# Four late-stage changes: order of the fold's first steps, engine of its high parts, theta's due time and conversion buffers

## The chip, the cores and the metric

One core of one Trainium2 chip runs the whole program in one launch. The metric is the time of the program on the device in microseconds (us). The core has a matmul engine (TensorE, PE in the profile, with its weight loads as PEld), VectorE (DVE), ScalarE (ACT), GpSimd (POOL), and SyncE (SP), which here issues nearly all transfers between memory (HBM) and the on-chip buffer SBUF. Matmuls write into PSUM, a small buffer that VectorE and ScalarE read.

## The reference

Two batches, 768 tokens, 8 heads of 64, model width 512. The three functions run one after the other on `x`; cut to what is computed:

```python
def _attn_ref(q, k, v, proj):
    ...
    q_bits = (np.einsum('bhsd,dk->bhsk', q, proj) > 0).astype(np.int64)
    k_bits = (np.einsum('bhsd,dk->bhsk', k, proj) > 0).astype(np.int64)
    powers = 2 ** np.arange(n_bits)
    q_bucket = np.sum(q_bits * powers, axis=-1)
    k_bucket = np.sum(k_bits * powers, axis=-1)
    mask = q_bucket[:, :, :, None] == k_bucket[:, :, None, :]
    scores = scale * np.matmul(q, k.transpose(0, 1, 3, 2))
    scores = np.where(mask, scores, -1000000000.0)
    scores = scores - np.max(scores, axis=-1, keepdims=True)
    attn = np.exp(scores)
    attn = attn / (np.sum(attn, axis=-1, keepdims=True) + 1e-09)
    return np.matmul(attn, v).astype(np.float32)

def _moe_ref(x, w_ch1, w_ch2):
    X = np.fft.fft(x, axis=1)
    X = np.fft.fft(X, axis=2)
    u = x + np.real(X).astype(np.float32)
    ...
    un = (u - mu) / np.sqrt(var + 1e-06)
    ch = np.maximum(un @ w_ch1, 0.0) @ w_ch2
    return (u + ch).astype(np.float32)

def _moe2_ref(x, w_theta, w_tok_r, w_tok_i, w_ch):
    theta = x @ w_theta
    zr, zi = x * np.cos(theta), x * np.sin(theta)
    y = np.einsum('ts,bsd->btd', w_tok_r, zr) + np.einsum('ts,bsd->btd', w_tok_i, zi)
    u = x + y
    return (u + np.maximum(u @ w_ch, 0.0)).astype(np.float32)
```

The MLP's and the second mixer's weights come as float64.

## The kernel before

The program is one stream of work for two batches of six tiles of 128 tokens each. First comes the attention of batch 0, in four pairs of heads (`attention_first`). Its last pair's second half is normalised by `pair_norm` into a PSUM piece `hi`, and ScalarE copies that to `x`. Then batch 0 goes through the transform (class `Fft`), the layernorm and the first MLP product (`mlp1`), while the attention of batch 1 runs beside it (48 tiles of scores, `exp`, transposes and products with `v`); then batch 0's second product (`mlp2`) and its `theta`, the same transform and MLP for batch 1, and last the second mixer of both batches: `theta(1, ...)`, the token sums `tok_sum` and the channel products `tok_out`, in halves of 384 tokens.

Most products are split: an operand is kept as a high and a low part (`xh`, `xl`; `w1h`, `w1l`), and three matmuls replace one.

The transform works on folded inputs. `fold` (l.568) adds and subtracts the upper and lower token tiles of `x` into `fm` (named `fa` in the trace), then column halves, and `part` (l.553) makes each of the pieces `z2`, `e`, `o`, `z0`: the sum or difference into PSUM (for the last pair of heads) or into `zraw`, a high part by ScalarE and a low part by VectorE. `fold` is a generator: each `yield` hands over to the attention's own steps. `rest` (l.614) then runs the matmuls with the tables `ct`, `sn` and `dt`, adds the results into `u`, and swaps two lone columns of each upper tile through a buffer `lone` (l.701 to 703). The layernorm of `u` follows, then `mlp1`.

Float64 weights are converted on the chip by `from_f64` (l.170): SyncE loads a slab of 512 (or 384) columns into a buffer `r64` (`r` in the trace); ScalarE makes two passes over it, VectorE joins the halves by a shift and an or; then ScalarE copies the high part and GpSimd subtracts to get the low part. The buffers come from a pool `cv` of three, in rotation (the list `cvs`). So are made `w1`, `w2`, the token weights (`conv_tok`: 12 tiles of 384 columns for each half, ten of them in the space of `w1`, the last two in `wtx`) and the channel weights `wch` (four tiles).

`theta` (l.814) takes each token tile: four transposes into PSUM, a copy `xs` that is stored to memory for `tok_sum`, the parts `xh` and `xl`, twelve matmuls, then range reduction, sine and cosine on the other engines. `tok_sum` (l.864) adds over 72 matmuls for each 128 channels; `tok_out` (l.886) does the last product, and stores.

What sets the order: each piece of code runs under a priority in microseconds, `at(us)`, or `timed(generator, t0, dt)` that gives the generator's steps the priorities t0, t0 + dt and so on. A scheduler places instructions by these, and by their dependencies; after that every engine runs its instructions strictly in that order, and SyncE's transfers are issued in such an order too. The numbers stand in the table `T` (l.93). Nearly every instruction is issued through one helper, so the trace names line 62 (or 64 for work whose order is kept as written) for all of them; they are told apart by their tiles' names.

Of the kernel before, what the change touches and what calls it, by code (L numbers as in the profile page):

```python
# [33 lines left out]
def f(t):  # L34
    return t.bitcast(F32)
# [35 lines left out]
def fused_kernel(ctx, tc, A, out):  # L71
# [15 lines left out]
    def stt(eng, out, in0, in1, op, scale=1.0):  # L87
# [8 lines left out]
        w2=100.0, w2s=1.0, m0=170.0, f1=190.0, th=240.0, m1=290.0, z0=330.0, wt=300.0, n0=8, n1=16, k0=12, k1=16, c1=46, i0=40, i1=[20, 10],  # L96
# [29 lines left out]
    def PS1():  # L126
        return PS(now[0])
# [262 lines left out]
    def pair_norm(j, part, o, hi=None):  # L390
# [8 lines left out]
        if hi is not None:  # L399
            AC.activation(out=x, in_=hi, func=AF.Copy)  # L400
# [54 lines left out]
    def attention_first(pace, after):  # L455
# [7 lines left out]
        def av(n):  # L463
# [5 lines left out]
            if i == NT - 1:  # L469
                hi = PS("m")[:, 0:384].rearrange("p (t a c) -> p t a c", t=3, a=2) if j == 3 and part else None  # L470
                pair_norm(j, part, o[0], hi)
                if part:
                    slow.append(after(j, hi))
# [57 lines left out]
    class Fft:  # L531
# [23 lines left out]
        def part(self, nm, c, op, a, b, psum=False):  # L555
# [9 lines left out]
            AC.activation(out=hl[:, 0], in_=r, func=AF.Copy)  # L565
            V.tensor_tensor(out=hl[:, 1], in0=r, in1=f(hl[:, 0]), op=ALU.subtract)

        def fold(self, p, hi=None):
# [11 lines left out]
            if hi is not None:  # L580
                fl = PS1()[:, 0:384].rearrange("p (a n) -> p a n", a=6)
# [35 lines left out]
        def rest(self):  # L617
# [64 lines left out]
            for t in range(3):  # L682
# [19 lines left out]
                AC.activation(out=mid, in_=u[:, 3 + t, 448:191:-256], func=AF.Copy)  # L702
                AC.activation(out=u[:, 3 + t, 192:449:256], in_=mid, func=AF.Copy)
# [110 lines left out]
    def theta(b, wth, zt):  # L814
        x2 = u_t[b]
        for t in range(NT):
# [4 lines left out]
            xs = zt([128, 4, 128], F32, "xs")  # L821
            AC.activation(out=xs, in_=pt.rearrange("p (k n) -> p k n", k=4), func=AF.Copy)
            SY.dma_start(out=xTd[b][:, :, c], in_=xs)
# [4 lines left out]
            V.tensor_tensor(out=xl, in0=pk, in1=f(xh), op=ALU.subtract)  # L828
            xx = (xh, xl)
# [59 lines left out]
    def tok_out(b, half, wch, kx):  # L889
# [3 lines left out]
        for m in range(4):  # L893
# [7 lines left out]
            if m % 2:  # L901
                SY.dma_start(out=out[b, 128 * m - 128:128 * m + 128, c].rearrange("(k p) t -> p k t", p=128),
                             in_=xt[:, m - 1:m + 1])
# [23 lines left out]
    attention_first(T["pace0"], lambda j, hi: ft0.fold(PO[j], hi))  # L927
# [100 lines left out]
    w2_p.release()  # L1028
    z1_p = pool("z1")
# [14 lines left out]
    timed(theta(1, wth, zt), t0, 1)  # L1044
# [25 lines left out]
    timed(tok_out(0, 1, wch, k1), t0 + 100, 1)  # L1070
    for p in (xt1_p, wc_p, zb_p, u1_p, xt_p, wx_p, z1_p, dr_p, ring["f"][0][0], ring["m"][1][0], ring["m"][0][0], w1_p, x_p, u0_p, cv_p, const):
        p.release()
# [101 lines left out]
```

## Time and profile before

| what | value |
|---|---|
| time, median of three runs | 740.17 us (737.42, 740.17, 740.52) |
| the profiled execution | 742.22 us |
| its span in the trace | 740.5 us |
| PE busy | 672.8 us, 91% |
| DVE busy | 401.4 us, 54% |
| ACT busy | 376.4 us, 51% |
| POOL busy | 371.2 us, 50% |
| chain that ended last | PE 42%, issue 10%, POOL 10%, DMA 9%, ACT 6%, DVE 4% |

The span is the time from the first to the last thing that the profiler recorded of this one execution; the execution's own time is a little longer. A row of the timeline has the start, the duration, the engine, the line, the operation and its tiles (output, arrow, inputs), and, where the engine was idle before it, how long and who released it. Idle time of an engine counts only where the work that ends last waits for it; in this kernel that is mostly TensorE's.

### The profile page before, as it was taken

The page shows a single profiled execution, that of the slowest core. Times are in us where ns is not written, and L with a number is a line of the kernel's source. Part 1 is how long each engine was busy: PE and PEld are TensorE (multiplying, and loading weights), DVE is VectorE, ACT ScalarE, POOL GpSimd, SP SyncE. Part 2 cuts the span into 40 slices and gives each one's busy share as a digit, 9 for nine tenths or more (in the row PEclk, how much of TensorE's full clock was granted, in tenths as well). Part 3 has the DMA queues.
Part 4 walks back from the last instruction along what each step waited for, and adds up shares of the span by engine and source line. Part 5 has one row for each costly group of instructions (what it writes and reads, how often), then busy time and mean ns, then how long its engine had stood idle before and what let it go on. Part 6 is the DMA issues. An engine that isn't in the chain of part 4 may idle for free.

```text
span 740.5 us, 13468 instructions
## 1 busy us (share of the span) xinstructions
PE 672.8 (91%) x5424; PEld 515.0 (70%) x5424; DVE 401.4 (54%) x649; ACT 376.4 (51%) x603; POOL 371.2 (50%) x312
## 2 busy tenths in 40 slices
PE   5798988778868897999999999999999799989997
PEld 2365566666747654786687675686584798989997
DVE  1466777778899556642394871254321366552222
ACT  2465554867898788764222260354325555562000
POOL 2777879589687888885450110134313155831000
PEclk9999999969789999999999999999999999999999
DMA  9886867469799999786550160010005511561202
GB/s 331 183 167 145 154 115 143 97 176 202 194 227 232 237 235 263 153 142 117 107 175 1 29 165 1 15 43 15 1 2 152 181 44 30 178 185 49 86 1 85
DMA packets 161438, 93.69 MB, mean 127 GB/s; under 512 B 137056, under 2 KB 147552, under 8 KB 161376
## 3 DMA queue, kind: packets, MB, share of 16 engines
q1 hardware_dynamic: 159440, 86.27, 49.9%
q0 software_dynamic: 1936, 6.57, 2.5%
q8 instruction: 42, 0.69, 0.4%
q14 instruction: 20, 0.16, 0.1%
HBM read 49.82 MB, written 6.29 MB: 76 GB/s over the span
## 4 chain that ended last, share of the span: by engine, by line
PE 42%; issue 10%; POOL 10%; DMA 9%; ACT 6%; DVE 4%; SPq 0%; POOLq 0%; ACTq 0%; DVEq 0%
PE psm L62 28%; PE psf L62 10%; DMA r<-in_wtok 4%; DMA r<-in_w 2%; POOL w1l L62 2%; ACT r L62 2%; POOL p L62 2%; PE pss L62 2%; POOL pt L62 2%; PE pso L62 2%; DMA r<-in_wch 1%; DMA x<-p 1%; ACT p L62 1%; ACT stk L62 1%; POOL w2l L62 1%
## 5 line engine op out<-in xcount | busy, mean ns | idle before, releaser
L62 PE MATMUL psm<-unT,w1h 128*128 128x256 f16 x768 | 130.1, 274 | 1.6 <-DVE u L62 1.4
L62 DVE SCALAR_TENSOR_TENSOR r<-r 128x512 uint32<-128x512 uint32 (+1 forms) x64 | 66.7, 1047 | 73.3 <-ACT r L62 61.4
L62 PE MATMUL psm<-unT,w1l 128*128 128x256 f16 x384 | 105.1, 274 | 0.0
L62 PEld LDWEIGHTS <-w1h 128*128 128x128 f16 (+1 forms) x774 | 75.2, 98 | 17.2 <-issue 6.3
L62 POOL TENSOR_TENSOR w1l<-r,w1h 128x384 fp32r<-128x384 f32 (+1 forms) x36 | 41.4, 1163 | 59.0 <-ACT w1h L62 58.9
L62 PEld LDWEIGHTS <-hh 128*128 128x128 f16 x384 | 36.9, 98 | 42.7 <-issue 1.1
L62 ACT ACTIVATE r<-r,chalf 128x512 uint32<-128x512 uint32 (+1 forms) x64 | 46.1, 721 | 38.3 <-DMA r<-in_wtok 20.5
L64 PE MATMUL pss<-stk 64*128 64x384 f32 (+1 forms) x288 | 58.4, 492 | 5.9 <-ACT p L64 3.0
L62 PE MATMUL pss<-stk 128*128 128x384 f32 x192 | 50.0, 388 | 11.9 <-ACT stk L62 6.6
L62 POOL TENSOR_TENSOR p<-p,p 128x768 f16<-128x768 f32 x32 | 53.4, 1672 | 12.9 <-ACT p L62 11.4
L62 PE MATMUL psm<-w2h,hl 128*128 128x512 f16 x192 | 59.7, 380 | 0.0
L62 PE MATMUL psm<-w2l,hh 128*128 128x512 f16 x192 | 59.4, 379 | 0.0
L62 PE MATMUL psm<-w2h,hh 128*128 128x512 f16 x192 | 59.3, 380 | 0.0
L62 DVE TENSOR_REDUCE nm<-pss 128x1 f32<-128x768 f32 x48 | 44.9, 946 | 20.5 <-PE pss L62 20.4
L64 DVE TENSOR_REDUCE nm<-pss 128x1 f32<-128x768 f32 x48 | 43.6, 950 | 22.5 <-PE pss L64 22.5
L62 ACT ACTIVATE p<-pss,nm 128x768 f32<-128x768 f32 x48 | 42.7, 895 | 21.7 <-DVE nm L62 20.2
L62 DVE SCALAR_TENSOR_TENSOR hl<-psm,hh 128x512 f16<-128x512 f32 x48 | 32.9, 685 | 37.8 <-ACT hh L62 37.7
L62 ACT ACTIVATE hh<-psm 128x512 f16<-128x512 f32 x48 | 28.3, 590 | 46.5 <-PE psm L62 46.4
L62 PEld LDWEIGHTS pss<-stk 128*128 128x128 f32 x192 | 35.3, 209 | 15.8 <-ACT stk L62 7.7
L62 PEld LDWEIGHTS <-w1l 128*128 128x128 f16 x384 | 37.6, 98 | 6.4 <-issue 1.7
L62 ACT ACTIVATE r<-r 128x512 f32<-128x512 f32 (+1 forms) x64 | 39.6, 619 | 0.0
L62 POOL TENSOR_SCALAR nn<-nn 128x512 f32<-128x512 f32 x12 | 8.3, 691 | 60.9 <-ACT nn L62 60.9
(319 smaller groups left out, 1583.8 us busy)
## 6 DMA issues: line engine op xcount, KB each, us to landing
r<-in_w SPq DMA_DIRECT2D x32, 512.0 KB, 4.9
r<-in_wtok SPq DMA_DIRECT2D x24, 384.0 KB, 3.8
vr<-in_v SPq DMA_DIRECT2D x8, 390.0 KB, 3.7
stk<-stk SPq DMA_DIRECT2D x16, 192.0 KB, 3.7
xT<-xs SPq DMA_DIRECT2D x12, 256.0 KB, 2.6
xt<-xT SPq DMA_DIRECT2D x4, 768.0 KB, 5.1
out<-xt SPq DMA_DIRECT2D x8, 384.0 KB, 2.5
ct<-in_ct POOLq DMA_DIRECT2D x4, 579.0 KB, 7.7
```

The costliest lines, as they stand in the source:

```text
L62: return fn(*a, **k)
L64: self.last = fn(*a, **k)
```

## The change

Eight edits, in four groups.

1. **Fold of batch 0's last pair.** `pair_norm` no longer issues the copy of `hi` to `x` itself but returns it as `back`; `fold` issues it after its first two additions. In `part`, where the piece is in PSUM (this pair only: four pieces), VectorE makes the high part, and ScalarE no longer does.
2. **Lone columns.** For batch 0 and its first tile the two copies of the swap are VectorE's.
3. **Tail.** In `theta`, the copy `xs` and its store are written behind `xh` and `xl`. The priorities of `theta(1, ...)` are 16 us earlier (`tp=16`). After the second MLP's weights are released, a pool `cv3` of three more buffers joins `cvs`, so that conversions from then on rotate over six. The program's ring for software DMA is 4096 bytes per partition where it had the default (`dynamic_dma_scratch_size`).
4. **End.** The last `tok_out` stores each 128 channels by itself (four stores of 128x384) where it stored two at a time.

```diff
@@ T = dict(...
-        ... k0=12, k1=16, c1=46, i0=40, i1=[20, 10],
+        ... k0=12, k1=16, c1=46, tp=16, i0=40, i1=[20, 10],
@@ pair_norm
-        if hi is not None:
-            AC.activation(out=x, in_=hi, func=AF.Copy)
+        return lambda: AC.activation(out=x, in_=hi, func=AF.Copy)
@@ attention_first, av
-                pair_norm(j, part, o[0], hi)
+                back = pair_norm(j, part, o[0], hi)
                 if part:
-                    slow.append(after(j, hi))
+                    slow.append(after(j, hi, back))
@@ class Fft, part
-            AC.activation(out=hl[:, 0], in_=r, func=AF.Copy)
+            if psum:
+                V.tensor_copy(out=hl[:, 0], in_=r)
+            else:
+                AC.activation(out=hl[:, 0], in_=r, func=AF.Copy)
             V.tensor_tensor(out=hl[:, 1], in0=r, in1=f(hl[:, 0]), op=ALU.subtract)
-        def fold(self, p, hi=None):
+        def fold(self, p, hi=None, back=None):
...
             yield
             if hi is not None:
+                back()
                 fl = PS1()[:, 0:384].rearrange("p (a n) -> p a n", a=6)
@@ class Fft, rest
-                AC.activation(out=mid, in_=u[:, 3 + t, 448:191:-256], func=AF.Copy)
-                AC.activation(out=u[:, 3 + t, 192:449:256], in_=mid, func=AF.Copy)
+                if self.b or t:
+                    AC.activation(out=mid, in_=u[:, 3 + t, 448:191:-256], func=AF.Copy)
+                    AC.activation(out=u[:, 3 + t, 192:449:256], in_=mid, func=AF.Copy)
+                else:
+                    V.tensor_copy(out=mid, in_=u[:, 3 + t, 448:191:-256])
+                    V.tensor_copy(out=u[:, 3 + t, 192:449:256], in_=mid)
@@ theta
-            xs = zt([128, 4, 128], F32, "xs")
-            AC.activation(out=xs, in_=pt.rearrange("p (k n) -> p k n", k=4), func=AF.Copy)
-            SY.dma_start(out=xTd[b][:, :, c], in_=xs)
             xh = zt([128, 4, 128], F32R, "xh")
             xl = zt([128, 4, 128], F32R, "xl")
             pk = pt.rearrange("p (k n) -> p k n", k=4)
             AC.activation(out=xh, in_=pk, func=AF.Copy)
             V.tensor_tensor(out=xl, in0=pk, in1=f(xh), op=ALU.subtract)
+            xs = zt([128, 4, 128], F32, "xs")
+            AC.activation(out=xs, in_=pt.rearrange("p (k n) -> p k n", k=4), func=AF.Copy)
+            SY.dma_start(out=xTd[b][:, :, c], in_=xs)
@@ tok_out
-    def tok_out(b, half, wch, kx):
+    def tok_out(b, half, wch, kx, last=False):
...
-            if m % 2:
+            if last:
+                SY.dma_start(out=out[b, 128 * m:128 * m + 128, c], in_=xt[:, m])
+            elif m % 2:
@@ the tail, after the second MLP
     w2_p.release()
+    cv3_p = pool("cv3", 3)
+    cvs += [cv3_p] * 3
...
-    timed(theta(1, wth, zt), t0, 1)
+    timed(theta(1, wth, zt), t0 - T["tp"], 1)
...
-    timed(tok_out(0, 1, wch, k1), t0 + 100, 1)
+    timed(tok_out(0, 1, wch, k1, True), t0 + 100, 1)
@@ building the program
-    nc = _bacc.Bacc("TRN2", target_bir_lowering=False, num_devices=1)
+    nc = _bacc.Bacc("TRN2", target_bir_lowering=False, num_devices=1, dynamic_dma_scratch_size=4096)
```

The changed program's order of instructions on each engine differs from the old one's at many places. Three of them are shown, each before and after. A row has the source line, the operation, the output tile, an arrow, the input tiles and the size; the number behind a tile's name only tells tiles apart.

**First batch's `u` on VectorE.** `psm_2066` is the transform's result for tile 0, `u_1888` is batch 0's `u`, `r64_...` are weights under conversion, `nm_...` and `bits_...` belong to the second batch's attention, `bs_...` are the layernorm's statistics. Before:

```order
L62 SCALAR_TENSOR_TENSOR r64_1933<-r64_1933 128x512
L64 TENSOR_TENSOR fa_1986<-psm_2039,fa_1986 128x386
L64 TENSOR_TENSOR hlz2_2063<-psm_2053,hlz2_2063 128x384
L62 TENSOR_SCALAR bits_2697<-pss_2698 64x768
L62 SCALAR_TENSOR_TENSOR r64_1940<-r64_1940 128x512
L64 TENSOR_TENSOR u_1888<-u_1888,psm_2066 128x512 x2
L62 TENSOR_REDUCE nm_2714<-pss_2709 128x1
L62 SCALAR_TENSOR_TENSOR r64_1947<-r64_1947 128x512
L64 TENSOR_TENSOR u_1888<-un0_113,psm_2087 1x512
L64 BN_STATS bs_2104<-u_1888 128x6
```

After:

```order
L62 SCALAR_TENSOR_TENSOR r64_1933<-r64_1933 128x512
L64 TENSOR_TENSOR hlz2_2063<-psm_2053,hlz2_2063 128x384
L64 TENSOR_TENSOR u_1888<-u_1888,psm_2066 128x512 x2
L62 SCALAR_TENSOR_TENSOR r64_1940<-r64_1940 128x512
L64 TENSOR_TENSOR u_1888<-un0_113,psm_2087 1x512
L62 TENSOR_SCALAR bits_2697<-pss_2698 64x768
L62 TENSOR_REDUCE nm_2673<-pss_2668 128x1
L64 COPY lone_2098<-u_1888 128x2
L62 SCALAR_TENSOR_TENSOR r64_1947<-r64_1947 128x512
L62 TENSOR_REDUCE nm_2714<-pss_2709 128x1
L64 COPY u_1888<-lone_2098 128x2
L64 BN_STATS bs_2104<-u_1888 128x6
```

The two additions into `u` stand ahead of the shift of `r64_1940` and of one step of the attention; the two copies of the lone columns are new on this engine, with a shift and a reduction between them.

**The second batch's theta on TensorE.** `psm_6592` and `psm_6593` are the last results of the second MLP (weights `w2h`, `w2l`), `psm_6975` a token sum, `psf_6738` (after: `psf_6741`) theta's tile 0, with `xh_6734` and `xl_6735`. Before, the last rows of 29 matmuls of the token sum that stand between the MLP and theta:

```order
L62 MATMUL psm_6975<-w1l_6521,x_5416 128x384
L62 MATMUL psm_6975<-w1h_6520,za_5417 128x384
L62 MATMUL psm_6975<-w1h_6520,zb_5418 128x384
L62 MATMUL psm_6975<-w1l_6521,zb_5418 128x384
L62 MATMUL psf_6738<-wthh_5386,xh_6734 128x512
L62 MATMUL psf_6738<-wthl_5387,xh_6734 128x512
L62 MATMUL psf_6767<-ident_93,u1_5032 128x128 x3
L62 MATMUL psf_6738<-wthh_5386,xl_6735 128x512
```

After:

```order
L62 LDWEIGHTS hh_6302
L62 MATMUL psm_6593<-w2l_2190,hh_6302 128x512
L62 LDWEIGHTS hl_6303
L62 MATMUL psm_6592<-w2h_2189,hl_6303 128x512
L62 MATMUL psf_6741<-wthh_5386,xh_6734 128x512
L62 MATMUL psf_6741<-wthl_5387,xh_6734 128x512
L62 MATMUL psf_6770<-ident_93,u1_5032 128x128 x2
L62 MATMUL psf_6741<-wthh_5386,xl_6735 128x512
```

Theta's tile 0 has moved from behind the MLP and 29 matmuls of the token sum into the MLP's last group.

**The same place on VectorE and SyncE.** `u1_5032` is the second batch's `x` of the mixer; its two additions take the MLP's last results. `r64_6585` to `r64_6722` are token weights, the `r64_71..` of 512 columns are channel weights. VectorE before:

```order
L62 SCALAR_TENSOR_TENSOR r64_6585<-r64_6585 128x384
L62 SCALAR_TENSOR_TENSOR r64_6712<-r64_6712 128x384
L62 SCALAR_TENSOR_TENSOR r64_6719<-r64_6719 128x384
L62 SCALAR_TENSOR_TENSOR u1_5032<-psm_6592,u1_5032 128x512
L62 SCALAR_TENSOR_TENSOR u1_5032<-psm_6593,u1_5032 128x512
L62 TENSOR_TENSOR xl_6735<-psf_6726,xh_6734 128x512
L62 SCALAR_TENSOR_TENSOR r64_7143<-r64_7143 128x512
L62 SCALAR_TENSOR_TENSOR r64_7150<-r64_7150 128x512
```

VectorE after:

```order
L62 TENSOR_TENSOR xl_6776<-psf_6770,xh_6775 128x512
L62 SCALAR_TENSOR_TENSOR rr_6757<-nn_6754,psf_6741 128x512
L62 SCALAR_TENSOR_TENSOR rr_6757<-nn_6754,rr_6757 128x512
L62 SCALAR_TENSOR_TENSOR r64_7146<-r64_7146 128x512
L62 SCALAR_TENSOR_TENSOR r64_7153<-r64_7153 128x512
L62 TENSOR_SCALAR nn_6754<-rr_6757 128x512
L62 SCALAR_TENSOR_TENSOR rr_6757<-rr_6757,u1_5032 128x512
L62 SCALAR_TENSOR_TENSOR r64_7160<-r64_7160 128x512
L62 SCALAR_TENSOR_TENSOR rr_6798<-nn_6795,psf_6782 128x512
L62 SCALAR_TENSOR_TENSOR u1_5032<-psm_6592,u1_5032 128x512
L62 SCALAR_TENSOR_TENSOR u1_5032<-psm_6593,u1_5032 128x512
```

SyncE before:

```order
L62 DMA r64_6585<-in_wtok 128x768
L62 DMA r64_6712<-in_wtok 128x768
L62 DMA r64_6719<-in_wtok 128x768
L62 DMA r64_7143<-in_wch 128x1024
L62 DMA xt_6973<-xT0_129 128x4x384
L62 DMA xT1_130<-xs_6731 512x1x128
L62 DMA r64_7150<-in_wch 128x1024
L62 DMA r64_7157<-in_wch 128x1024
L62 DMA xT1_130<-xs_6772 512x1x128
```

SyncE after:

```order
L62 DMA xT1_130<-xs_6738 512x1x128
L62 DMA r64_6585<-in_wtok 128x768
L62 DMA r64_7146<-in_wch 128x1024
L62 DMA r64_7153<-in_wch 128x1024
L62 DMA xT1_130<-xs_6779 512x1x128
L62 DMA r64_7160<-in_wch 128x1024
L62 DMA r64_6715<-in_wtok 128x768
L62 DMA r64_6722<-in_wtok 128x768
L62 DMA xt_6976<-xT0_129 128x4x384
L62 DMA r64_7167<-in_wch 128x1024
L62 DMA r64_7340<-in_wtok 128x768
L62 DMA r64_7347<-in_wtok 128x768
```

On VectorE the two additions into `u1` now stand behind theta's steps of tiles 0 and 1 and behind the shifts of three channel tiles; on SyncE the load of the third of these, `r64_7160`, stands behind the store of tile 1's `xs_6779`, and the last two token tiles of the first half, `r64_6715` and `r64_6722`, come behind it.

## Rows read from the trace of the kernel before

**Rows 1.** Stretches: start:end, length, busy us by engine, PEclk, DMA share, GB/s.

```profile
120.00:300.00 180.00, 145.49 (x1410) 110.62 (x1411) 136.97 (x200) 144.56 (x222) 146.27 (x105) 0.89 0.89 203
...
300.00:560.00 260.00, 258.43 (x2033) 188.14 (x2031) 124.94 (x231) 101.03 (x166) 86.55 (x80) 1.00 0.31 71
...
560.00:620.00 60.00, 55.69 (x290) 44.50 (x287) 26.75 (x44) 33.64 (x63) 23.37 (x23) 1.00 0.33 104
...
640.00:680.00 40.00, 36.23 (x207) 35.60 (x206) 16.65 (x29) 19.91 (x40) 15.84 (x14) 1.00 0.50 157
...
680.00:720.00 40.00, 40.00 (x231) 40.00 (x230) 8.13 (x15) 2.63 (x5) 0.00 (x0) 1.00 0.12 40
```

**Rows 2.** What TensorE waited for, 560 to 740: us, times, longest.

```profile
PE psf L62 <- ACT xh L62: 4.5, 3, 2.2
PE psm L62 <- ACT w1h L62: 2.7, 1, 2.7
PE psm L62 <- DVE xt L62: 1.1, 1, 1.1
```

**Rows 3.** Timeline at the fold: start, us, engine, line, operation, tiles, [idle <-releaser].

```profile
141.07 0.57 DVE L64 TENSOR_TENSOR psm<-pso,r 128x384 f32<-128x384 f32 x1
...
147.58 0.49 ACT L64 ACTIVATE x<-psm 128x384 f32<-128x384 f32 x1
...
148.11 1.02 DVE L62 TENSOR_TENSOR fa<-x,psm 128x384 f32<-128x384 f32 x2 [0.37 <-ACT x L64]
...
151.45 2.93 PE L62 MATMUL pss<-stk 128*128 128x384 f32 x8 [2.86 <-ACT p L62]
...
155.99 3.26 PE L62 MATMUL psm<-ct,hlz 128*128 128x386 f32 x9 [1.61 <-DVE hle L62]
```

**Rows 4.** Timeline from the first batch's additions to its first MLP matmul.

```profile
177.94 2.10 POOL L62 TENSOR_TENSOR pt<-p,pt 128x768 f16<-128x768 f32 x1
...
178.47 4.84 DVE L62 SCALAR_TENSOR_TENSOR r<-r 128x512 uint32<-128x512 uint32 x1
...
183.24 1.27 DVE L64 TENSOR_TENSOR u<-u,psm 128x512 f32<-128x512 f32 x2
...
185.30 0.67 DVE L62 SCALAR_TENSOR_TENSOR r<-r 128x512 uint32<-128x512 uint32 x1
...
185.89 1.65 PE L62 MATMUL pss<-stk 128*128 128x384 f32 x4 [4.39 <-ACT stk L62]
...
188.04 0.20 ACT L62 ACTIVATE u<-lone 128x2 f32<-128x2 f32 x1
...
205.12 0.73 PE L62 MATMUL pso<-vv,x 128*128 128x65 f16 x18 [1.33 <-DMA x<-p]
...
212.05 1.65 PE L62 MATMUL pss<-stk 128*128 128x384 f32 x4 [0.77 <-ACT stk L62]
...
213.50 0.65 PE L62 MATMUL psm<-unT,w1h 128*128 128x256 f16 x2
```

**Rows 5.** Timeline at the second batch's theta.

```profile
573.49 0.65 ACT L62 ACTIVATE r<-r,chalf 128x384 uint32<-128x384 uint32 x1 [1.39 <-DMA r<-in_wtok]
...
580.07 0.59 ACT L62 ACTIVATE xh<-psf 128x512 fp32r<-128x512 f32 x1
...
580.71 0.50 PE L62 MATMUL psf<-wthh,xh 128*128 128x512 f32 x1 [1.87 <-ACT xh L62]
```

**Rows 6.** DMA issues: tiles, queue, count, KB each, us to landing.

```profile
r<-in_wtok SPq DMA_DIRECT2D x24, 384.0 KB, 3.8
...
out<-xt SPq DMA_DIRECT2D x8, 384.0 KB, 2.5
...
r<-in_wch SPq DMA_DIRECT2D x4, 512.0 KB, 5.4
```

**Rows 7.** Timeline of GpSimd: a low part in the loop of three buffers.

```profile
658.56 1.04 POOL L62 TENSOR_TENSOR w1l<-r,w1h 128x384 fp32r<-128x384 f32 x1 [4.18 <-ACT w1h L62]
```

**Rows 8.** Timeline of VectorE at the end of the program.

```profile
736.25 0.56 DVE L62 SCALAR_TENSOR_TENSOR xt<-psf,xt 128x384 f32<-128x384 f32 x1 [1.53 <-PE psf L62]
```

More of the change, by code (lines that the diff above doesn't have):

```diff
@@ L95, in fused_kernel @@
         lg=[[0, 2], [2, 4], [4, 6]], ub=2, pace0=1.6, lead=60, f0=50.0, w1=60.0, w1s=1.0, b1=115, pace1=2.6,
-        w2=100.0, w2s=1.0, m0=170.0, f1=190.0, th=240.0, m1=290.0, z0=330.0, wt=300.0, n0=8, n1=16, k0=12, k1=16, c1=46, i0=40, i1=[20, 10],
+        w2=100.0, w2s=1.0, m0=170.0, f1=190.0, th=240.0, m1=290.0, z0=330.0, wt=300.0, n0=8, n1=16, k0=12, k1=16, c1=46, tp=16, i0=40, i1=[20, 10],
         ne=42, es=150, ld='ss', lc='s', ps=[[0, 3], [0, 5], [1, 0], [1, 5]])
@@ L925, in fused_kernel @@
         ft0 = Fft(0, "left")
-    attention_first(T["pace0"], lambda j, hi: ft0.fold(PO[j], hi))
+    attention_first(T["pace0"], lambda j, hi, back: ft0.fold(PO[j], hi, back))
     al = [x for t in kept for x in one(t, *range(t.shape[1]))]
@@ L1069, in fused_kernel @@
     timed(tok_out(1, 1, wch, k0), t0 + 90, 1)
-    timed(tok_out(0, 1, wch, k1), t0 + 100, 1)
-    for p in (xt1_p, wc_p, zb_p, u1_p, xt_p, wx_p, z1_p, dr_p, ring["f"][0][0], ring["m"][1][0], ring["m"][0][0], w1_p, x_p, u0_p, cv_p, const):
+    timed(tok_out(0, 1, wch, k1, True), t0 + 100, 1)
+    for p in (xt1_p, wc_p, zb_p, u1_p, xt_p, wx_p, z1_p, cv3_p, dr_p, ring["f"][0][0], ring["m"][1][0], ring["m"][0][0], w1_p, x_p, u0_p, cv_p, const):
         p.release()
```

## The prediction

> **What bounds the kernel now.** The table of stretches comes first [rows 1]: one core, the granted clock at its upper level from 300 us on, and TensorE busy 258.43 of 260 us between 300 and 560. Nothing can be won in that middle but by doing less, and the change removes no matmul. What can be won is the time in which TensorE stands: 34.5 us of the 180 between 120 and 300 (180.00 − 145.49), 4.3 of the 60 from 560, 3.8 of the 40 from 640. The list of what TensorE waits for from 560 to 740 [rows 2] names all of the tail's: three waits for `xh`, 4.5 us together, one for a converted weight `w1h`, 2.7, and one for `xt`, 1.1. For the early stretch I read the timeline around the fold [rows 3] and around the first batch's `u` [rows 4]. The reader is to see there that the first batch's chain (fold, transform, `u`, layernorm, first MLP matmul) runs beside the second batch's attention, so that TensorE stands only where both are late.
>
> **Base.** The profiled execution took 742.22 us (span 740.5), 2.05 above the median of 740.17. I make the sum against 742.22 and take the same difference from the median.
>
> **Tail: theta of the second batch, 0.7 us (from −3 to +4.5).** Before, the three waits for `xh` cost 4.5 us [rows 2]; the first of them is 1.87 us at 580.71, directly behind the last MLP matmuls [rows 5]. Two edits act on it. `xh` is copied before `xs`, which saves one copy, about 0.6 us, on each tile's way (`xh` and `xs` have the same shape, and `xh` took 0.59 [rows 5]). And theta's due time comes 16 us earlier; in the order, tiles 0 and 1 now stand inside the last MLP group instead of behind it and 29 matmuls of the token sum. Tile 0 then waits for nothing: its `xh` comes early on ScalarE. Tile 1's `xh` stands behind the last converted tile of the token weights: ScalarE's first step for that tile runs from 573.49 for 0.65 [rows 5]; its second, theta's scaling and `xh` itself follow at about 0.55 to 0.7 each, so it ends near 576.0. The matmuls between need TensorE until about 574.8: a wait of 1.0 us. Tile 2 needs the last MLP result added into `u1` by VectorE, and here the order has a new trap: that addition now stands behind the shift of `r64_7160`, a tile of `in_wch` whose load is behind the store of tile 1's `xs` on SyncE's queue. That store can go at about 579.4; a wtok tile lands in 3.8 us, a wch tile in 5.4 [rows 6], so the tile is there between 583.2 and 584.8; two steps of ScalarE, its next one for theta, GpSimd's rounding and VectorE's three (0.6 to 0.7 each) lead to about 587.9. TensorE would want tile 2 near 585.1: a wait of 2.8 (0 if the load is quick and the token sum's matmuls cover it, 5 if the load is slow). So 4.5 − 1.0 − 2.8 = 0.7.
>
> **Tail: weights of the token sum, 3.8 us (2 to 4).** Three conversion buffers make a loop: load, two steps of ScalarE, VectorE's shift, ScalarE's high part, GpSimd's low part, and only then the next load. Its mark is the low part at 658.56 that came 4.18 us after GpSimd was free [rows 7]; TensorE then waits the 2.7 for `w1h` and, through the same ring of tiles, 1.1 for `xt` [rows 2]. With six buffers the four wch tiles and the first wtok tiles of the second half are loaded some ten us earlier, while the engines that convert are half free (ScalarE 19.91 of 40 us, GpSimd 15.84 [rows 1]). From 680 on TensorE is busy 40.00 of 40, so nothing else is late right behind. I take both waits as gone, 3.8. The three new buffers lie where the second MLP's weights lay, so the last two wtok tiles of the first half cannot load before that MLP ends, near 580.5; they are wanted near 592, and a load of 3.8 us with the conversion's 4 fits.
>
> **Last stores, 0.2 us (0 to 0.6).** The span ends 3.7 us after VectorE's last addition (736.25 + 0.56 to 740.5) [rows 8]. Four stores of 192 KB replace two of 384 KB, which landed in 2.5 us [rows 6]; part of that may be size, most is not, since a wtok tile of the same 384 KB took 3.8.
>
> **Early: fold, `u` and layernorm of the first batch, 2.0 us (from −4.4 to +6).** `back`: VectorE's product was ready at 141.64, ScalarE's copy came at 147.58, and the first two additions at 148.11 [rows 3]: they waited 6.5 us for a copy that they don't read (they read the PSUM piece). Now the copy is behind them. But the transform's matmuls at 155.99 stand behind eight matmuls of scores at 151.45, which wait 2.86 for an `exp` [rows 3], and that stays: I count the transform 1 us earlier. The four high parts move from ScalarE (it copies 384 columns in 0.49 [rows 3], so under 2 us for the four) to VectorE. The trace has no such cast; its nearest row is the 0.57 for a 128x384 product out of PSUM [rows 3], so between 1.5 and 2.3 us, on an engine that idles there: nothing. The larger part is `u`: its two additions at 183.24 stood behind a shift of 4.84 us, where the same shift took 0.67 at 185.30 [rows 4]. In the new order they stand ahead of that shift, so `u` and its statistics come 3 to 5 us sooner, and the swap of the two lone columns loses two hops between engines (ScalarE's copies took 0.20 each [rows 4]). What that brings on TensorE is bounded by the waits ahead of the first MLP matmul at 213.50: four of them, from the 1.33 at 205.12 to the 0.77 at 212.05, 4.3 us in all [rows 4]; the MLP's matmuls can stand in these. I fill about half, 2.0. The upper end takes all and a little of the stretches behind; the lower end is another wait like the 4.39 at 185.89 [rows 4].
>
> **The rest.** The smaller ring for software DMA makes room and costs nothing: the few transfers that use it start long before any stretch of this sum.
>
> **Sum.** 0.7 + 3.8 + 0.2 + 2.0 = 6.7: 742.22 becomes 735.5, the median 740.17 − 6.7 = 733.5. Its own range is 730.5 to 736.5.
>
> **The rivals.** *All comes at once* (729): the load of `r64_7160` is quick, so 2.8 more, and the early waits are filled whole, 2.3 more: 6.7 + 5.1 = 11.8, less some 0.7 for waits that move on, 11.1. For it: the middle is full of work that can be drawn forward. Against it: a late tile 2 stands in the order. Chance 0.14. *Only the weights* (737.0): theta's wait for tile 2 is as long as the three waits before, and the early chain ends at the same `exp` and transposes as before (the waits at 205 to 212 are the second batch's); 3.8 − 0.6 = 3.2. Chance 0.27. *The buffers don't help* (739.5): they come free too late, the loop keeps its beat, and TensorE waits as before; against it are 60 us between 580 and 640. Chance 0.05. *VectorE stalls beside GpSimd* (744): the shift of 4.84 us at 178.47 ran beside GpSimd's 2.10 us at 177.94 and cost 4.2 more than its 0.67 [rows 4]. The change gives VectorE more to do in just that stretch, where GpSimd is busy 146.27 of 180 us [rows 1], and puts the two lone copies, SBUF to SBUF, ahead of the layernorm. If each meets such a stall, 8.4 us come in, the early 2.0 is gone, and 8.4 − 4.7 = 3.7 is lost: 743.9. It decides from two whole stalls on; one leaves 740. Against it: the casts and additions read PSUM, and the copies have two elements per row. Chance 0.08.
>
> The Trainium skill has a rule that speaks for the last rival: in "SBUF — State Buffer", section "Who interferes with whom", it says that a VectorE instruction with two SBUF inputs contends with a GpSimd instruction that reads SBUF, and that VectorE's `copy` and `cast` can take the port pair which both share, with the later one fully blocked. The shift's row agrees (two SBUF inputs, 4.84 against 0.67 us). By that rule a lone copy waits out at most one GpSimd instruction, here 2.10 us, so two of them 4.2 and the sum would be 2.5 instead of 6.7; I keep 6.7, as no row shows a copy that waits.
>
> **Numbers.** Forecast 0.46, then 0.14, 0.27, 0.05, 0.08. A measurement of this kernel tells about 0.5% (3.7 us) from no change, so the bounds are 736.5 and 743.9. Faster: 0.46 + 0.14 and 0.05 of the third case, 0.65; slower: 0.08; the same: 0.27. The range goes from 727 to 741 and leaves out the last rival and a little of the first.
>
> **What would show it.** The fold's first additions at 142 to 143 rather than 148; the first MLP matmul 3 to 5 us before 213.5; waits of TensorE for `xh` of about 1 and 3 us instead of three of 4.5; TensorE full from 640 to 680, and low parts on GpSimd without gaps of 4 us. I am wrong if a wait for `u1` or a new buffer of over 5 us stands near 585, or if the first MLP matmul has not moved.

## The result, and the profile after

The changed kernel takes 728.66 us (median of four runs, 728.28 to 730.17) beside 740.0 us for the kernel before: a ratio of 0.9845, 95% interval 0.9815 to 0.9875, or 11.3 us less. The forecast was 733.5 with a range of 727 to 741; the direction and the range held, and the gain is 1.7 times the forecast's 6.7. It lies nearest to the rival "all comes at once" (729), but not by that rival's mechanism, as will be seen.

The profiled execution took 728.28 us. Its page begins, with the busy time of each engine:

```profile
span 726.5 us, 13450 instructions
...
PE 664.8 (92%) x5424; PEld 510.9 (70%) x5424; DVE 402.6 (55%) x655; ACT 372.7 (51%) x597; POOL 370.1 (51%) x312
```

Three of the stretches of [rows 1]; columns are the stretch, its length, busy us of PE, PEld, DVE, ACT, POOL, then the granted clock, DMA share, GB/s:

```profile
560.00:620.00 60.00, 57.78 (x306) 49.45 (x305) 36.01 (x54) 41.28 (x77) 30.82 (x30) 1.00 0.41 126
640.00:680.00 40.00, 40.00 (x233) 40.00 (x232) 12.48 (x22) 4.50 (x9) 2.52 (x2) 1.00 0.14 49
680.00:720.00 40.00, 40.00 (x230) 40.00 (x230) 8.37 (x15) 2.10 (x4) 0.00 (x0) 1.00 0.16 55
```

From 640 on TensorE is full (it lacked 3.8 us before), and from 560 to 620 it stands 2.2 us instead of 4.3. What TensorE waited for in the tail, 545 to 726.5, is one line where [rows 2] had three:

```profile
PE psf L62 <- DVE u L62: 2.2, 1, 2.2
```

**Where the 14.0 us between the two profiled spans lie.** Three landmarks stand in both traces: the last `exp` of the first batch's attention on ScalarE, the last matmul group of the second batch's first MLP product (552.18 before, 546.22 after), and the last matmul group (735.87, 722.61). Before, and then after:

```profile
128.95 0.90 ACT L64 ACTIVATE p<-pss,nm 128x768 f32<-128x768 f32 x1
...
552.18 0.38 PE L62 MATMUL psm<-unT,w1h 128*128 128x256 f16 x2
...
735.87 0.34 PE L62 MATMUL psf<-u,wchl 128*128 128x384 f32 x1
```

```profile
125.36 0.89 ACT L64 ACTIVATE p<-pss,nm 128x768 f32<-128x768 f32 x1
...
546.22 0.38 PE L62 MATMUL psm<-unT,w1h 128*128 128x256 f16 x2
...
722.61 0.34 PE L62 MATMUL psf<-u,wchl 128*128 128x384 f32 x1
```

So 3.6 us are gone before any moved instruction has run (the orders of all engines are equal up to there), 2.4 between the first and the second landmark (423.2 against 420.9), 7.3 in the tail (183.7 against 176.4), and 0.7 behind the last matmuls (4.6 against 3.9). The first of these goes with the granted clock. Before, in two stretches from 90 to 140 us (length, busy time of PE, granted clock, DMA share, GB/s):

```profile
90.00:110.00 20.00, 16.69 (x207) 0.91 0.64 113
110.00:140.00 30.00, 26.02 (x360) 0.89 0.63 119
```

and after:

```profile
90.00:110.00 20.00, 16.21 (x215) 1.00 0.68 126
110.00:140.00 30.00, 23.85 (x396) 1.00 0.64 123
```

At 0.91 and 0.89 a part of the stretch ran at the lower level (1.2 GHz), at 1.00 all of it at the upper (2.4 GHz), with the same instructions in the same order. The profiled execution of before lay 2.2 us above its kernel's median and that of after 0.4 below its own; that is the difference between the 14.0 us of the two profiles and the 11.3 of the medians.

### The profile page after: what moved, and what is told of

It is laid out like the page before. It is cut to its first block, busy times and chain, and to the rows that moved or that the text cites. A ratio compares the mean times of both kernels' runs of the same rounds, so it can differ in the third digit from the quotient of the medians.

```text
span 726.5 us, 13450 instructions
## 1 busy us (share of the span) xinstructions
PE 664.8 (92%) x5424; PEld 510.9 (70%) x5424; DVE 402.6 (55%) x655; ACT 372.7 (51%) x597; POOL 370.1 (51%) x312
## 4 chain that ended last, share of the span: by engine, by line
PE 48%; POOL 10%; issue 9%; DMA 6%; ACT 5%; DVE 4%; POOLq 0%; SPq 0%; DVEq 0%; ACTq 0%
PE psm L62 31%; PE psf L62 14%; POOL p L62 3%; ACT r L62 2%; PE pso L62 2%; POOL w1l L62 2%; DMA x<-p 2%; POOL stk L62 2%; PE pss L62 1%; DMA r<-in_wtok 1%; DMA r<-in_w 1%; POOL pt L62 1%; DVE r L62 1%; ACT stk L62 1%; POOL w2l L62 1%
## 5 line engine op out<-in xcount | busy, mean ns | idle before, releaser
L62 DVE SCALAR_TENSOR_TENSOR r<-r 128x512 uint32<-128x512 uint32 (+1 forms) x64 | 64.6, 1016 | 51.9 <-ACT r L62 49.2
L64 PE MATMUL pss<-stk 64*128 64x384 f32 (+1 forms) x288 | 55.4, 470 | 6.4 <-ACT p L64 3.2
L62 POOL TENSOR_TENSOR stk<-tt,stk 64x768 fp32r<-64x768 f32 x16 | 31.1, 1945 | 11.5 <-issue 9.6
```

What stands on the lines that cost most here:

```text
L62: return fn(*a, **k)
L64: self.last = fn(*a, **k)
```

## Experiments: the two halves

In each, the profile was read at the three landmarks. The table gathers them, with PE's waits of the tail; "first to second" is from the last `exp` to the last group of the MLP product, "tail" from there to the last matmul group, all in us. Ratios are to the kernel before on the same chip, with their 95% intervals; medians of different rows were partly taken on different chips. The kernels in the lower rows are explained below.

| kernel | median | ratio | last exp at | first to second | tail | PE waits in the tail |
|---|---|---|---|---|---|---|
| before | 740.0 | 1 | 128.9 | 423.2 | 183.7 | 8.3 |
| before_again | 739.4 | 1.0007 (0.9981 to 1.0033) | 127.9 | 421.7 | 185.3 | 7.1 |
| changed | 728.7 | 0.9845 (0.9815 to 0.9875) | 125.4 | 420.9 | 176.4 | 2.2 |
| tail_only | 734.8 | 0.9918 (0.9890 to 0.9947) | 130.0 | 423.7 | 176.9 | 2.5 |
| early_only | 735.5 | 0.9947 (0.9914 to 0.9981) | 123.5 | 420.6 | 187.1 | 8.7 |
| no_cv3 | 731.3 | 0.9879 (0.9847 to 0.9911) | 125.9 | 421.3 | 178.6 | 3.0 |
| no_tp | 730.2 | 0.9896 (0.9871 to 0.9921) | 127.9 | 421.5 | 177.6 | 2.6 |
| xs_first | 731.2 | 0.9905 (0.9876 to 0.9933) | 128.1 | 418.9 | 179.1 | 3.7 |
| no_last | 730.0 | 0.9881 (0.9847 to 0.9915) | 123.0 | 422.0 | 178.2 | 2.4 |
| u1_first | 732.2 | 0.9894 (0.9863 to 0.9924) | 124.3 | 422.8 | 179.5 | 4.2 |
| wch_t2 | 728.4 | 0.9848 (0.9811 to 0.9884) | 124.3 | 421.1 | 176.6 | 2.1 |
| no_back | 739.2 | 0.9994 (0.9962 to 1.0027) | 124.1 | 430.6 | 176.7 | 2.6 |
| no_part | 740.1 | 1.0013 (0.9986 to 1.0040) | 124.6 | 435.4 | 178.2 | 2.3 |
| no_lone | 733.7 | 0.9915 (0.9880 to 0.9951) | 124.7 | 424.8 | 178.4 | 2.5 |

How far one profile can be trusted is seen on two rows. In no_last all engines run the changed kernel's order up to the last stores, and still it takes 422.0 and 178.2 us where the changed kernel takes 420.9 and 176.4, some 3 us more from the last `exp` to the last matmul. A smaller difference of these lengths between two single profiles shows nothing by itself.

**tail_only**: the changed kernel without its early edits.

```diff
+                if hi is not None:
+                    back()
...
-            if psum:
-                V.tensor_copy(out=hl[:, 0], in_=r)
-            else:
-                AC.activation(out=hl[:, 0], in_=r, func=AF.Copy)
+            AC.activation(out=hl[:, 0], in_=r, func=AF.Copy)
...
-                    V.tensor_copy(out=mid, in_=u[:, 3 + t, 448:191:-256])
-                    V.tensor_copy(out=u[:, 3 + t, 192:449:256], in_=mid)
```

> The changed kernel with its early edits undone: the copy of `hi` to `x` at once, the high parts of the fold and the lone columns by ScalarE again; the edits of the tail stay. Theory (tail 6.1 us of waits and 0.7 of the last store; early 3.1 us; the 2.8 us by which the profile of after is ahead at 121 us, where the orders are still equal, are the clock of that one execution): 732 to 733 us, and the first MLP matmul at about 213. Rival 1 (the early edits bring nothing, and all of what the profiles show there is the clock): 728.7 us, as after. Rival 2 (the early edits bring the whole 6.0 us by which after is ahead at the last MLP): 734.5 us.

**early_only**: the kernel before with the three early edits and nothing of the tail (the diff of the section on the change, its groups 1 and 2).

> The kernel before with the early edits alone: the copy of `hi` to `x` behind the fold's first additions, the four high parts and the first tile's lone columns by VectorE. Theory: 740.0 - 3.1 = 737 us, with TensorE's waits of the tail (for `xh`, `w1h`, `xt`, together 8.3 us) as before. Rival 1 (nothing early): 740 us. Rival 2 (6 us early): 734 us.

Measured: the tail alone takes 6.1 us off (0.9918 of 740; by its interval 3.9 to 8.1), the early edits alone 3.9 (1.4 to 6.4). Together that is 10.0, and the whole change brings 11.5 (9.3 to 13.7): within these intervals the halves add up. For the tail the theory held in its waits, which are those of the changed kernel (2.5 against 2.2 us, from 8.3), and so did its time within the interval, though the interval (731.9 to 736.1 of 740) holds rival 2's 734.5 as well. The early half lies between the theory and rival 2, and rival 1 (nothing) is outside its interval.

The traces don't show where an early gain lies. From the first to the second landmark the old early order takes 423.2, 421.7 and 423.7 us (three profiles), the new one 418.9 to 422.8 (eight, mean 421.1), 1.8 us less; but from the last `exp` to the last matmul early_only takes 607.7 us where the kernel before takes 606.9 and 607.0 in its two profiles. Its span is shorter only by what lies ahead of the last `exp`, where no instruction has moved. Between tail_only (600.6) and the changed kernel (597.3) there are 3.3 us, hardly more than the 3 between two executions of one order. Nor are waits filled: in the 420 us behind the last `exp` PE was busy 385.81 us before and 386.12 after, so it stood 34.2 and 33.9 us:

```profile
128.95:548.95 420.00, 385.81 (x3302) 286.94 (x3299) 252.81 (x419) 238.60 (x375) 221.06 (x173) 0.96 0.55 125
```

```profile
125.36:545.36 420.00, 386.12 (x3324) 287.47 (x3321) 248.81 (x426) 236.55 (x370) 220.85 (x174) 0.96 0.56 126
```

**before_again**: the kernel before, unchanged, to see whether the late last `exp` belongs to the old fold.

> The kernel before, unchanged, for a second profile. In the profiles of before and of the kernel without early edits the last `exp` of the first batch's attention came at 129 and 130 us, in the eight others at 123 to 126, though the instructions up to there stand in the same order in all. Theory (it is the granted clock of one execution): here between 123 and 130, most likely about 125. Rival (something in the programs with the old fold that the order doesn't show): again 129 to 130.

It came at 127.90, and at 127.93 and 128.12 in no_tp and xs_first, which have the new early order:

```profile
127.90 0.89 ACT L64 ACTIVATE p<-pss,nm 128x768 f32<-128x768 f32 x1
```

```profile
127.93 0.90 ACT L64 ACTIVATE p<-pss,nm 128x768 f32<-128x768 f32 x1
```

The theory's likeliest value (about 125) missed, though 127.90 is within its 123 to 130, and the rival's "129 to 130" missed too; what decides is that two kernels with the new order show the late `exp` as well, with the granted clock of before to the hundredth. The stretches of no_tp:

```profile
90.00:110.00 20.00, 16.64 (x210) 0.91 0.67 118
110.00:140.00 30.00, 26.13 (x373) 0.89 0.65 119
```

So the old fold is not needed for this clock. But all three profiles of the old early order have it (0.91 and 0.90 in tail_only), and only two of the eleven with an early edit. Another rival is the chip: three of the five late ones are among the four profiles of one chip (no_tp, xs_first, before_again and, not late, no_last). The clock isn't all of it either: where it was 1.00, the last `exp` still came anywhere from 122.98 to 125.91. Which of these holds was not tested, and with it stays open whether the measured early gain belongs to the edits or to the clock of these executions.

The second profile of the unchanged kernel shows one thing more. The shift that took 4.84 us in [rows 4] took 1.44 here, and `u` and its first statistics followed 51.0 and 54.4 us behind the last `exp`, against 54.3 and 57.5 in the first profile:

```profile
177.15 1.44 DVE L62 SCALAR_TENSOR_TENSOR r<-r 128x512 uint32<-128x512 uint32 x1
...
178.90 1.28 DVE L64 TENSOR_TENSOR u<-u,psm 128x512 f32<-128x512 f32 x2 [0.31 <-PE psm L62]
...
182.28 0.67 DVE L64 BATCH_NORM_STATS2 bs<-u 128x6 f32<-128x512 f32 x1
```

In tail_only, which has the same early order, it took 4.70. So the stall comes and goes with the execution.

## Experiments: the early edits one by one

Each undoes one edit in the changed kernel: no_back copies `hi` to `x` ahead of the fold again, no_part makes the four high parts by ScalarE again, no_lone the first tile's lone columns.

```diff
# no_back
                 back = pair_norm(j, part, o[0], hi)
+                if hi is not None:
+                    back()
...
-                back()
# no_part
-            if psum:
-                V.tensor_copy(out=hl[:, 0], in_=r)
-            else:
-                AC.activation(out=hl[:, 0], in_=r, func=AF.Copy)
+            AC.activation(out=hl[:, 0], in_=r, func=AF.Copy)
# no_lone
-                if self.b or t:
-                    AC.activation(out=mid, in_=u[:, 3 + t, 448:191:-256], func=AF.Copy)
...
+                AC.activation(out=mid, in_=u[:, 3 + t, 448:191:-256], func=AF.Copy)
```

> The changed kernel with the copy of `hi` to `x` again ahead of the fold. Early theory 1 (the early gain of 5 to 6 us between the kernels with and without early edits comes from the fold's first additions): 733 to 734 us. Theory 2 (it comes from the new interleaving of the second batch's attention with the MLP, to which each of the three edits gives a part): 730 to 732 us. Theory 3 (nothing of it is early, it is the clock): 728.7 us.

> The changed kernel with the fold's four high parts by ScalarE again. Theory 1 (the fold's additions carry the early gain, the high parts nothing): 729 us. Theory 2 (the interleaving, each edit a part): 730 to 732 us. Theory 3 (clock): 728.7 us.

> The changed kernel with the first tile's lone columns by ScalarE again. Theory 1 (as for the high parts): 729 us. Theory 2: 730 to 732 us. A theory of its own (a copy of VectorE that waits beside GpSimd, 0.92 us where the other took 0.15, delays the layernorm): 728 us, 0.8 us faster than the change.

For no_back and no_part all three theories fell; for no_lone they missed the median, though theory 2's 732 is within the interval (731.1 to 736.4 of 740). Undoing one edit costs 10.5, 11.4 and 5.1 us of the median, where undoing all three costs 6.1. The edits are not a sum of small terms: with one of them undone the scheduler makes yet another interleaving of the second batch's attention with the first batch's MLP (of the 5424 matmuls, some 1660 in no_back, 1550 in no_part and 700 in no_lone stand elsewhere than in the changed kernel), and those of no_back and no_part are worse than both the old and the new. no_part shows how: its first MLP matmul comes 81.0 us behind the last `exp`, earlier than the changed kernel's 85.6, and still the MLP's last group comes 14.5 us later. In its 420 us behind the `exp` PE is busy 377.73, so it stands 42.3 us instead of 33.9, which is 8.4 of the 14.5; no_back stands 41.0, 7.1 of its 9.7. (The profiled execution of no_part was 3.7 us above its median, that of no_back 2.1 below.) The stretch of no_part:

```profile
124.57:544.57 420.00, 377.73 (x3191) 276.85 (x3188) 254.02 (x416) 235.21 (x368) 220.69 (x174) 0.95 0.57 126
```

Which of the moved instructions makes these waits was not isolated.

In no_lone the fourth expectation was that the median falls by 0.8 us, since a copy by VectorE waits beside GpSimd. The copy does wait (below), but the median rose.

## Experiments: the tail's parts

**no_cv3** (three conversion buffers), **no_tp** (theta's old priority), **xs_first** (the old order of the copies), **no_last** (stores two at a time), each undone alone:

```diff
# no_cv3
-    cvs += [cv3_p] * 3
# no_tp
-        ... tp=16, ...
+        ... tp=0, ...
# no_last
-    timed(tok_out(0, 1, wch, k1, True), t0 + 100, 1)
+    timed(tok_out(0, 1, wch, k1), t0 + 100, 1)
# xs_first
+            xs = zt([128, 4, 128], F32, "xs")
+            AC.activation(out=xs, in_=pt.rearrange("p (k n) -> p k n", k=4), func=AF.Copy)
+            SY.dma_start(out=xTd[b][:, :, c], in_=xs)
             xh = zt([128, 4, 128], F32R, "xh")
...
```

> The changed kernel with three conversion buffers as before (the room for the other three is kept, but they are not used). Theory (the buffers took away the waits for `w1h` and `xt`): 728.7 + 3.8 = 732.5 us, with those two waits of 2.7 and 1.1 us back, and perhaps 1 to 2 us less at theta's tile 2, since the third channel tile is loaded later and its shift stands behind the additions into `u1`; then 731. Rival (theta's earlier place drew the conversions ahead, the buffers did nothing): 728.7 us and no wait for `w1h`.

> The changed kernel with theta of the second batch at its old priority. Theory (its earlier place takes away the waits for `xh`; what is left is the 2.2 us for `u1`): the waits for `xh` of 3 to 4.5 us come back, the 2.2 us go: 730 to 731 us. Rival (the six buffers alone shorten theta's waits too, since ScalarE's conversions are no longer late): 728.7 us or less, with waits for `xh` under 2 us.

By the medians no_cv3 costs 2.7 and no_tp 1.5 us, by the ratios 2.5 and 3.8, with intervals that overlap the changed kernel's. In neither did the 2.7 us for `w1h` come back. What PE waited for in the tail of no_cv3:

```profile
PE psf L62 <- ACT xh L62: 0.9, 2, 0.6
PE psf L62 <- DVE xl L62: 0.8, 1, 0.8
PE psf L62 <- DVE u L62: 0.5, 1, 0.5
PE psm L62 <- POOL wtx L62: 0.5, 1, 0.5
PE psm L62 <- DVE xt L62: 0.3, 1, 0.3
```

and of no_tp:

```profile
PE psf L62 <- ACT xh L62: 1.3, 1, 1.3
PE psf L62 <- DVE xl L62: 0.8, 1, 0.8
PE psm L62 <- ACT wtx L62: 0.5, 1, 0.5
```

So no_cv3's time (731.3) is near the theory's 731, but its waits are the rival's; and in no_tp the wait for `u1` went, as the theory had it, while the waits for `xh` stayed under 2 us, as the rival had it. Neither edit is needed for the weights of the token sum as long as the other is there. In no_cv3 the loop of three buffers keeps its beat, with GpSimd's low parts up to 3.4 us apart, but it starts sooner: the second half's first low part comes at 626.56, 79.4 us behind the second landmark, where it came 88.7 behind it before (640.87):

```profile
648.57 1.07 POOL L62 TENSOR_TENSOR w1l<-r,w1h 128x384 fp32r<-128x384 f32 x1 [3.44 <-ACT w1h L62]
```

Both kernels also have the new order of `xh` and `xs`; no run has that order without both, so a part of it in this is not excluded. What each edit still adds, beside the other, is under 1 us of waits (3.0 and 2.6 against 2.2); the tails (178.6 and 177.6 us) differ from 176.4 by about as much as no_last's 178.2 does.

> The changed kernel with `xs` and its store again ahead of `xh`. Theory (TensorE waits for theta only at tile 2, for `u1`, which hangs on a load behind the store of tile 1's `xs`; so the order of the two copies brings nothing now, and an earlier store even helps): 728 to 729 us. Rival (a copy of 0.6 us on each tile's way): 729.3 to 731 us, with waits for `xh`.

The rival was nearer: 731.2 (0.9905, its interval just above the changed kernel's), with waits for `xh` of 1.1 us, 1.2 for `u1` and a new one of 1.4 for `za`.

> The changed kernel with the last product's stores two at a time. Theory (the profiles' 0.74 us between the last matmul and the end is the size of the last store): 729.4 us, and 4.6 us from the last matmul's start to the end instead of 3.9. Rival (hidden or fixed cost): 728.7 us.

The theory held: from VectorE's last addition (723.56 + 0.56) to the end (727.8) it takes 3.7 us, as in [rows 8], and 3.0 in the changed kernel (722.98 + 0.56 to 726.5); tail_only, which also has the smaller store, takes 3.0 too. The addition in no_last, and then in the changed kernel:

```profile
723.56 0.56 DVE L62 SCALAR_TENSOR_TENSOR xt<-psf,xt 128x384 f32<-128x384 f32 x1 [1.53 <-PE psf L62]
```

```profile
722.98 0.56 DVE L62 SCALAR_TENSOR_TENSOR xt<-psf,xt 128x384 f32<-128x384 f32 x1 [1.53 <-PE psf L62]
```

The median of 730.0 agrees, though its interval reaches down to the changed kernel's.

**u1_first and wch_t2** go after the one wait that was left in the tail. The timeline of the changed kernel shows it as the prediction drew it: a store, the load of the third channel tile behind it, ScalarE, VectorE's shift, the addition into `u1`, TensorE:

```profile
571.75 0.52 SPq L62 DMA_DIRECT2D xT<-xs  x1
572.37 0.58 SPq L62 DMA_DIRECT2D r<-in_wch  x1
...
576.69 0.76 ACT L62 ACTIVATE r<-r,chalf 128x512 uint32<-128x512 uint32 x1 [1.37 <-DMA r<-in_wch]
...
577.89 0.67 ACT L62 ACTIVATE nn<-psf,cmag 128x512 f32<-128x512 f32 x1
...
578.03 0.69 DVE L62 SCALAR_TENSOR_TENSOR r<-r 128x512 uint32<-128x512 uint32 x1 [2.60 <-ACT r L62]
579.30 0.69 DVE L62 SCALAR_TENSOR_TENSOR rr<-nn,psf 128x512 f32<-128x512 f32 x1 [0.58 <-POOL nn L62]
579.91 1.28 DVE L62 SCALAR_TENSOR_TENSOR u<-psm,u 128x512 f32<-128x512 f32 x2
...
580.65 0.66 PE L62 MATMUL psf<-ident,u 128*128 128x128 f32 x4 [2.22 <-DVE u L62]
```

u1_first orders the conversion of the channel weights behind the additions:

```diff
-    timed(conv32(A["wch"], ...), t0 + 22, 1)
+    with after_gate("u1"):        # "u1": the last addition into u1
+        timed(conv32(A["wch"], ...), t0 + 22, 1)
```

> The changed kernel with the conversion of the channel weights ordered behind the additions into `u1`. Theory (TensorE's wait of 2.2 us for `u1` at 580 comes from the shift of the third channel tile, whose load stands behind a store of `xs`): 728.7 - 2.2 = 726.5 us, and no wait of over 0.5 us there. Rival (theta's tile 1, whose rounding on GpSimd also stands ahead of these additions, is as late, or the channel weights then come late): 728.7 us, with a wait of 1.5 to 2.5 us in either place.

The rival held, and more: a wait of 2.20 us for `u1` stayed, 1.4 for `xh` came. The edit put only the conversion's steps on VectorE behind the additions. VectorE's shift was out of the way, but ScalarE, in order, still stood for that load, and behind it theta's scaling of tile 1, which GpSimd and VectorE need ahead of `u1`. u1_first:

```profile
577.91 0.75 ACT L62 ACTIVATE r<-r,chalf 128x512 uint32<-128x512 uint32 x1 [2.60 <-DMA r<-in_wch]
...
580.53 0.69 DVE L62 SCALAR_TENSOR_TENSOR rr<-nn,psf 128x512 f32<-128x512 f32 x1 [5.10 <-POOL nn L62]
...
581.87 0.66 PE L62 MATMUL psf<-ident,u 128*128 128x128 f32 x4 [2.20 <-DVE u L62]
```

wch_t2 orders the same conversion behind `xh` of theta's tile 2, on ScalarE, so that neither queue stands for the load:

```diff
-    timed(conv32(A["wch"], ...), t0 + 22, 1)
+    with after_gate(("xh", 2)):   # the copy `xh` of theta's tile 2
+        timed(conv32(A["wch"], ...), t0 + 22, 1)
```

> The changed kernel with the conversion of the channel weights ordered behind `xh` of theta's tile 2. With the additions into `u1` ahead, TensorE still waited 2.2 us for `u1`, and ScalarE stood 2.6 us for the load of the third channel tile with theta's tile 1 queued behind it. Theory (that load holds ScalarE's queue, and through it the rounding of tile 1 and `u1`): now no engine waits for it there, the wait for `u1` goes, 728.7 - 2.2 = 726.5 us. Rival (tile 1's chain through GpSimd is late by itself): a wait of about 2 us for `u1` stays, 728.7 us or more.

The wait for `u1` is gone, so the load was its cause, through ScalarE. The time is not: 728.4 against 728.7. PE's waits in the tail of wch_t2 are now:

```profile
PE psf L62 <- DVE za L62: 1.6, 1, 1.6
PE psf L62 <- ACT xh L62: 0.5, 1, 0.5
```

The wait has moved. TensorE comes sooner to the last `za`, but VectorE starts that no sooner (87.7 us behind the second landmark, 87.5 in the changed kernel), and beside a GpSimd subtraction it took 1.51 us where it took 0.68:

```profile
633.09 1.51 DVE L62 SCALAR_TENSOR_TENSOR za<-nn,u 128x512 fp32r<-128x512 f32 x1
```

No kernel here is faster than the changed one by more than the measurement's uncertainty.

## Why the prediction was right, and where not

The forecast held because of the tail: its three terms, 4.7 us together, were measured as 6.1 (3.9 to 8.1) by tail_only. The fourth, early, came out larger than forecast, and not by its mechanism.

**Theta, predicted 0.7, measured 2.3 in waits** (1.0 against the second profile of before, whose waits for `xh` were 3.2). Tile 0 waits for nothing, as said. Tile 1, for which 1.0 was counted, waits for nothing either. For tile 2 the mechanism was drawn as it happened, the store at 571.75 ahead of the load included, and sized 2.8 where it is 2.2. The step named VectorE's shift as the trap and counted ScalarE's steps behind the load as well; u1_first and wch_t2 show that ScalarE's are the ones that decide. In the changed kernel too the shift ends at 578.72 and VectorE's next step starts at 579.30, when GpSimd's rounding, behind ScalarE, releases it.

**Weights, predicted 3.8, measured 3.8, for a reason only half right.** Both waits are gone. But the step that gave them to the buffers alone failed: without the buffers they stay away. With theta's move (and the new order of `xh` and `xs`) the same loop starts early enough.

**Last stores, predicted 0.2, measured 0.7.** The step "part of that may be size, most is not" compared a store with a load of the same size; with the store of half the size the span ends 2.9 to 3.0 us behind the last addition (ten profiles), with the old one 3.6 to 3.7 (four): 0.7 us, a little above the bound of 0.6.

**Early, predicted 2.0.** The first additions of the fold came at 139.66, 14.3 us behind the last `exp` (19.2 before), and the additions into `u` at 176.30, 50.9 behind it (54.3 before), as expected. Nothing came of either. The transform starts 27.1 us behind the `exp` after and 27.0 before (the prediction counted it 1 us earlier), and the first MLP matmul at 210.93, 85.6 us behind it, is 1.0 later, not 3 to 5 sooner. The timeline after, on VectorE, with TensorE's first MLP matmul at its end, shows where the lead of `u` went:

```profile
176.30 1.29 DVE L64 TENSOR_TENSOR u<-u,psm 128x512 f32<-128x512 f32 x2 [1.88 <-PE psm L62]
...
180.43 0.15 DVE L64 COPY lone<-u 128x2 f32<-128x2 f32 x1
...
181.97 0.92 DVE L64 COPY u<-lone 128x2 f32<-128x2 f32 x1
182.80 0.68 DVE L64 BATCH_NORM_STATS2 bs<-u 128x6 f32<-128x512 f32 x1
183.40 3.00 DVE L62 SCALAR_TENSOR_TENSOR r<-r 128x512 uint32<-128x512 uint32 x1
...
210.93 0.38 PE L62 MATMUL psm<-unT,w1h 128*128 128x256 f16 x2
```

Ahead of the swap stand a reduction and a step of the second batch's attention; the second copy is stretched; and the shift that was passed (4.84 us in [rows 4]) meets another one of 3.00 right behind the first statistics. The failed step is "`u` and its statistics come 3 to 5 us sooner": `u` did, the statistics did not (the first is 57.4 us behind the `exp`, 57.5 before). And the stall that it was to pass is not a fixed cost: the unchanged kernel's second profile has 1.44 us in its place, `u` at 51.0 and the statistics at 54.4 without any edit. Nor do sooner statistics make the MLP sooner by themselves: in no_lone they come at 53.6, and the first MLP matmul at 85.6, as in the changed kernel. The waits of TensorE there were not filled; they were 34.2 us in the 420 behind the `exp` and are 33.9. That the measured early half is 3.9 us (1.4 to 6.4) all the same is not explained by this step: the traces show no gain behind the last `exp` that is clear of the 3 us between executions, and what is ahead of it stands where no instruction has moved. That this term had the right sign is luck as far as the runs show.

**The rival of VectorE beside GpSimd (744, chance 0.08)** is there in kind and small in size. The second copy took 0.92 us where the first took 0.15, and ended at 182.89, with the GpSimd subtraction that had begun at 180.98:

```profile
180.98 1.88 POOL L62 TENSOR_TENSOR stk<-tt,stk 64x768 fp32r<-64x768 f32 x1 [0.84 <-ACT stk L62]
```

In seven other kernels with this edit the second copy took 0.91 to 0.93 as well, in no_back 1.63, and in no_part 0.17:

```profile
182.94 0.17 DVE L64 COPY u<-lone 128x2 f32<-128x2 f32 x1
```

The Trainium skill, "SBUF — State Buffer", section "Who interferes with whom", says that such a copy can take the ports that VectorE shares with GpSimd, and that whoever comes later blocks fully; here the trace agrees, with 0.77 us lost on one copy of two. The prediction kept 0 for it, and its price is below 1 us.

**"The buffers don't help"** (739.5, chance 0.05) fell: with six buffers the loop lost its beat, GpSimd's `w1l` of the second half standing at most 0.8 us apart, and both waits are gone. Only that the waits go without the buffers too speaks for it. The smaller ring for software DMA was not tried alone; no wait points to it.

## What to carry to other kernels

Where a scheduler places the work, an edit's price is that of the whole order that it leads to: undoing single edits here cost up to twice what undoing all of them cost, so a bundle should be split on the chip before its parts are credited. A late load in an in-order queue has to be followed on every engine that touches the tile, since taking one of them out of the way leaves the next. And two profiles should be laid on each other at landmarks that stand ahead of the change, to see first how far they differ before the change can act; and a second profile of an unchanged order tells which stalls are fixed and which come and go.

## What the runs showed of the hardware

With the same instructions in the same order on every engine, the first batch's attention takes one of two courses: in 5 of 14 profiles the granted clock was 0.91 from 90 to 110 us and 0.89 or 0.90 from 110 to 140, in the others 1.00 there, and the last `exp` came at 127.9 to 130.0 us in the former, 123.0 to 125.9 in the latter (4.2 us between the means). A shift on VectorE with GpSimd at work beside it took 4.84 us in one execution and 1.44 in another of the same program. From the last `exp` to the last matmul two executions with one order of instructions (the changed kernel and no_last) took 597.3 and 600.2 us. A store of 192 KB at the very end lets the span end 0.7 us sooner than one of 384 KB (3.0 against 3.7 us behind the last addition). And a copy of 128x2 elements, SBUF to SBUF on VectorE, took 0.92 us instead of 0.15 when a GpSimd subtraction ran.
